# First pair of q and k through another queue and in float32, and the bias table's copies split in two, in an attention and feed-forward kernel

## The chip, the core and the metric

The kernel runs on one core of one Trainium2 chip. A core has a matrix engine (TensorE, called PE in the profile, its weight loads PEld), VectorE (DVE), ScalarE (ACT), GpSimd (POOL) and SyncE (SP), each with an instruction queue of its own, and 16 DMA engines that they share. The metric is the time of one execution on the device in microseconds (us), the lower the better. Times before and after are medians of several runs.

## The reference

Attention with a relative-position bias, over 8 batches, 8 heads, 576 positions and 64 numbers a head, and then a feed-forward stage over the 4608 tokens of 512 numbers:

```python
scores = scale * np.matmul(q, k.transpose(0, 1, 3, 2))
bias = bias_table[bucket]                    # 32 buckets x 8 heads, bucket depends on |i - j|
scores = scores + bias.transpose(2, 0, 1)[None, :, :, :]
attn = np.exp(scores - np.max(scores, axis=-1, keepdims=True))
attn = attn / (np.sum(attn, axis=-1, keepdims=True) + 1e-09)
x = np.matmul(attn, v)                       # heads side by side: 4608 x 512
h = x @ w_in                                 # 512 -> 2048
out = np.maximum(0.01 * h, h) @ w_out        # 2048 -> 512
```

All inputs and the output are float32. Beyond a distance of 127 the bucket, and so the bias, is the same for all.

## The kernel before, in words

The work is cut into 32 items, one for each batch and pair of heads (`items`, L244). The loop at L485 goes through them in order; item n's scores are made, item n-1's are multiplied with v, item n+1's q and k are turned, and pieces of the feed-forward stage (`moe`, L449) are strewn between, as soon as four pairs of a batch have given finished tokens. The order on each engine is that of the program text (`manual_schedule`, L68): an engine that waits for one instruction holds up all that stand behind it.

An item takes these steps:

- `load_qk` (L108) brings q and k of some heads by a DMA of GpSimd's queue, which casts to bfloat16 on the way, into `qn` and `kn`: 96 partitions, 6 rows of each head in a partition. `load_v` (L130) does the same for v.
- `pair_rows` (L251) sets the two heads of a pair side by side in a tile `pr`, with one VectorE copy for q and one for k (L256).
- `turned_pair` (L266) turns `pr` with six small matmuls (L272) into PSUM; `transpose_k` (L289) and `transpose_q` (L283) copy that into `kt` and `qt` (L291 on VectorE; L286 on ScalarE for the first pair), and `apart` (L276) makes a masked copy of the last 64 columns on VectorE (L278).
- `qk_mm` (L294) multiplies, `exp_band` (L315) takes the exponential on ScalarE (L319, L321, L326), and `band` (L330) multiplies the result on VectorE by a band of factors around the diagonal (L344): the bias as exp(bias - last bias), which is 1 outside of the band. For items 0 and 1 the bands come late: `bands(0)` stands at L540, near the end of the loop's second round, followed by `av(0, 0)` and `av(0, 1)`, and `bands(1)` at L550.
- `av` (L346) multiplies with v into one PSUM tile `ps_o` (one buffer), takes the reciprocal (L362) and scales (L363) on VectorE.

The factors come from the bias table. `tabT` is loaded on SyncE's queue (L170). VectorE negates its last column (`negc`, L182), ScalarE takes the exponential (`e8`, L183), and VectorE spreads the 32 values over a row `ub` of 512 places: one copy for the first 16 (L186), 15 copies for the runs of the others (L189), and one mirrored copy (L194). The row goes to DRAM as `u_row` (L200, SyncE), and from there three sorts of loads on SyncE's queue bring it back with one place's shift in each partition: `hk` for heads 0 and 1 (L202), `hk4` in two halves (L209, for the last 64 keys of every head, used by `band` with u = 5), and `hk` for heads 2 to 7 (L202).

`spin(k)` (L471) issues k matmuls on a tile of zeros, whose result is not used. The program has `spin(11)` ahead of the first pair (L479) and `spin(5)` behind its transposes (L484). ScalarE's first instructions are a table load and an exponential of one number (L85).

Of the kernel before, what the change touches and what calls it, by code (L numbers as in the profile page):

```python
# [10 lines left out]
FP32 = mybir.dt.float32  # L11
BF16 = mybir.dt.bfloat16
# [6 lines left out]
def bucket_runs(n_buckets, max_distance, seq):  # L19

    half = n_buckets // 2
    n = np.arange(seq)
    lr = np.log(np.maximum(n, 1).astype(np.float32) / half) / np.log(max_distance / half)
    large = np.minimum(half + (lr * (half - 1)).astype(np.int32), n_buckets - 1)
    bucket = np.where(n < half, n, large)
    assert (bucket[max_distance:] == n_buckets - 1).all()
    runs = []
    for d in range(max_distance):
        u = int(bucket[d])
        if runs and runs[-1][0] == u:  # L30
            runs[-1][2] = d
        else:
            runs.append([u, d, d])
    return runs
# [3 lines left out]
def kernel(  # L38
# [69 lines left out]
    def load_qk(b, h0, h1):  # L108
        i = b % NBUF
        for src, dst in ((q, qn[i]), (k, kn[i])):  # L110
            nc.gpsimd.dma_start(
                out=dst[0:RQ, h0:h1, :, :].rearrange("r h c d -> r h (c d)"),
                in_=src[b, h0:h1, :, :].rearrange("h (r c) d -> r h (c d)", c=NC),
            )
# [51 lines left out]
    for e in range(2):  # L166
        nc.vector.memset(own[e * D : (e + 1) * D, e, :], 1.0)
    tabT = per.tile([H, NB], FP32, name="tabT")
    with nc.allow_non_contiguous_dma(reason="a table of 256 numbers"):
        nc.sync.dma_start(out=tabT, in_=bias_table.rearrange("u h -> h u"))  # L170
    load_qk(0, 0, 2)
    make_identity(nc, ident)


# [8 lines left out]
    nc.scalar.activation(e8, tabT, AF.Exp, bias=negc[:, 0:1], scale=1.0)  # L183
    C0 = 2 * P - 1
    small = NB // 2
    nc.vector.tensor_copy(out=ub[:, C0 : C0 + small], in_=e8[:, 0:small])  # L186
    for u, lo, hi in bucket_runs(NB, BAND, S):
        if lo >= small:
            nc.vector.tensor_copy(  # L189
                out=ub[:, C0 + lo : C0 + hi + 1],  # L190
                in_=e8[:, u : u + 1].to_broadcast([H, hi - lo + 1]),
            )
    row = ub[:, :]
    nc.vector.tensor_copy(  # L194
        out=ub[:, C0 - BAND + 1 : C0],
        in_=bass.AP(tensor=row.tensor, offset=row.offset + C0 + BAND - 1,
                    ap=[list(row.ap[0]), [-1, BAND - 1]]),
    )
    udr = nc.dram_tensor("u_row", [H, UW], BF16, kind="Internal")
    nc.sync.dma_start(out=udr.ap(), in_=ub)  # L200
    def load_hk(h0, h1):
        nc.sync.dma_start(  # L202
            out=hk[:, h0:h1, :],
            in_=bass.AP(tensor=udr, offset=h0 * UW, ap=[[1, P], [UW, h1 - h0], [1, BW]]),
        )

    load_hk(0, 2)
    for e in range(2):
        nc.sync.dma_start(  # L209
            out=hk4[e * SL : (e + 1) * SL, :, :],  # L210
            in_=bass.AP(tensor=udr, offset=e * UW + SL + P, ap=[[1, SL], [2 * UW, n_pairs], [1, P + SL]]),
        )
    load_hk(2, H)

    def mirrored(t, lo, hi):

# [3 lines left out]
        ap[-1][0] = -1  # L220
        return bass.AP(tensor=v.tensor, offset=v.offset + hi - lo - 1, ap=ap)

    load_qk(0, 2, 4)
    load_qk(0, 4, 6)
    clear_edges(nc.vector, 1)
    load_v(0, 0, 2, True)
    load_qk(0, 6, H)
    load_v(0, 2, H, False)
# [22 lines left out]
    def pair_rows(n):  # L251

        b, p = items[n]
        t = prs[n] = pr_pool.tile([RQ, 2, NC, 2 * D], BF16, name="pr")
        for j, src in enumerate((qn, kn)):
            nc.vector.tensor_copy(out=t[:, j, :, :].rearrange("r c (e d) -> r c e d", e=2),  # L256
                                  in_=src[b % NBUF][0:RQ, 2 * p : 2 * p + 2, :, :].rearrange("r e c d -> r c e d"))

    def by_dma(n):
        return n >= 2 * n_pairs + 2  # L260
# [125 lines left out]

    def ffn_in(T):
        t0 = T * TT
        gt = gts[T] = gt_pool.tile([P, n_fc, TT], BF16, name="gt")
        for f in range(n_fc):  # L390
            pm = ps_m_pool.tile([P, TT], FP32, name="pm1", tag="m")
            for c in range(n_cc):
                nc.tensor.matmul(pm, lhsT=w_in_sb[:, c, f * P : (f + 1) * P], rhs=xT[c][:, t0 : t0 + TT],  # L393
                                 start=(c == 0), stop=(c == n_cc - 1))
            nc.scalar.activation(gt[:, f, :], pm, AF.Prelu, bias=0.0, scale=1.0, alpha=0.01)
            yield
# [79 lines left out]
        for u in range(NJ + 2):  # L476
            band(n, u)

    spin(11)  # L479

    pair_rows(0)
    transpose_k(0)
    transpose_q(0)
    spin(5)  # L484
    for n in range(N + 1):  # L485
        live = n < N
        if live:
            b, p = items[n]
            if n == 0:
                load_w_in(0)  # L490
                load_v(1, 0, H, False)
                load_w_in(1)
                load_w_out(0)
                load_w_out(1)
            elif 0 < b < B - 1:
                if p < 2:
                    load_qk(b + 1, 4 * p, 4 * p + 4)
                if p > 0:
                    load_v_part(b + 1, p - 1)
            if n + 1 < N and not by_dma(n + 1):  # L500
                pair_rows(n + 1)
            if n + AHEAD < N and by_dma(n + AHEAD):
                pair_rows(n + AHEAD)
                turn_by_dma(n + AHEAD)
            ps_a, ps_b = qk_mm(n, 0), qk_mm(n, 1)
            exp_band(n, 0, ps_a)
# [78 lines left out]
```

## Time and profile before

| what | value |
|---|---|
| runs | 391.61, 393.40, 393.59 us; median 393.4 us |
| span of the profiled execution, first to last instruction | 435.3 us |
| mean granted TensorE clock in it | 0.852 |
| PE, PEld busy | 421.2 us (97%), 199.4 us (46%) |
| DVE, ACT, POOL busy | 209.3 us (48%), 242.2 us (56%), 69.0 us (16%) |
| DMA queue q0 (GpSimd's) | 53664 packets, 18.36 MB, 40.5% of the 16 engines' span |
| DMA queue q1 (SyncE's) | 49912 packets, 21.02 MB, 26.8% |

For the profiled execution only the span is given; it stands for its own time, and it is 41.9 us above the median of the runs. The page of the profile divides the span into 40 slices and lists busy time, queues and groups of instructions. The timeline lists instructions by their start, in us from the span's start, with the time that they took; where one row stands for several instructions, xN is their number and the time is from the start of the first to the end of the last, as far as they follow each other. In brackets stands how long the engine sat idle before, and what ended that. "SPq" is SyncE's queue issuing a DMA; "KB, us" in a row on a DMA is the size at its destination and the time from the issue to the landing. The chain of waits is followed back from the last instruction to what released it.

### The profile page before, as it was taken

How to read it: one execution, taken by the hardware profiler on the slowest of the kernel's cores; microseconds unless marked ns; L12 is line 12 of the kernel's file. 1: busy time of each engine (PE TensorE's matmuls, PEld its weight loads, DVE VectorE, ACT ScalarE, POOL GpSimd, SP SyncE). 2: the span in 40 equal slices, each digit the busy share in tenths (PEclk: the TensorE clock that was granted, in tenths of full speed). 3: DMA queues.
4: the chain of work that ended last, by engine and by line, in shares of the span. 5: the costliest groups of instructions: out<-in, count | busy, mean ns of one | idle time of the engine just before them, and what ended most of it. 6: DMA issues, size and time to landing. Idle time of an engine off the chain costs nothing.

```text
span 435.3 us, 8219 instructions
## 1 busy us (share of the span) xinstructions
PE 421.2 (97%) x3384; PEld 199.4 (46%) x3384; DVE 209.3 (48%) x551; ACT 242.2 (56%) x343; POOL 69.0 (16%) x100
## 2 busy tenths in 40 slices
PE   8777999999999999999999999999999999999996
PEld 3445555444444444444444444444444454444442
DVE  6588557764556455555555455545554320000111
ACT  4776776576645666476646764676457713354000
POOL 8834230420051002400060004000000000000000
PEclk9888888888888888888888888888888888888888
DMA  8999992999289714974399349522422010000111
GB/s 107 194 196 197 206 168 42 106 131 146 64 82 172 113 27 81 185 123 44 68 152 171 44 68 98 115 37 54 60 65 17 24 43 24 26 24 0 74 48 72
DMA packets 103613, 39.89 MB, mean 92 GB/s; under 512 B 82576, under 2 KB 97944, under 8 KB 103576
## 3 DMA queue, kind: packets, MB, share of 16 engines
q0 software_dynamic: 53664, 18.36, 40.5%
q1 hardware_dynamic: 49912, 21.02, 26.8%
q8 instruction: 26, 0.43, 0.4%
q14 instruction: 11, 0.09, 0.1%
HBM read 37.68 MB, written 9.45 MB: 108 GB/s over the span
## 4 chain that ended last, share of the span: by engine, by line
PE 91%; DVE 5%; ACT 2%; issue 1%; ACTq 0%
PE ps_o L357 9%; PE ps_s L301 7%; PE ps_o L359 2%; PE ps_w L473 2%; PE ps_s L305 2%; PE ps_s L308 2%; DVE opair L363 1%; DVE at_113 L344 1%; PE pm_2157 L404 1%; PE pm_4504 L404 1%; PE pm_3930 L404 1%; PE pm_1566 L404 1%; PE pm_3339 L404 1%; PE pm_2748 L404 1%; PE pm_3191 L404 1%
## 5 line engine op out<-in xcount | busy, mean ns | idle before, releaser
L393 PEld LDWEIGHTS <-w_in_sb 128*128 128x128 bf16 x576 | 55.9, 104 | 75.6 <-issue 8.3
L404 PEld LDWEIGHTS <-gt 128*128 128x128 bf16 x576 | 54.2, 104 | 78.1 <-issue 15.0
L319 ACT ACTIVATE at_114<-ps_s 128x1024 bf16<-128x1024 f32 x64 | 62.9, 1023 | 29.4 <-PE ps_s L301 29.2
L319 ACT ACTIVATE at_113<-ps_s 128x1024 bf16<-128x1024 f32 x64 | 62.6, 1022 | 14.3 <-PE ps_s L301 14.1
L344 DVE TENSOR_TENSOR at_114<-at_114,hk 128x512 bf16<-128x512 bf16 (+1 forms) x64 | 32.2, 506 | 38.4 <-ACT at_114 L319 30.1
L344 DVE TENSOR_TENSOR at_113<-at_113,hk 128x512 bf16<-128x512 bf16 (+1 forms) x64 | 32.0, 506 | 37.9 <-ACT at_113 L319 33.7
L357 PEld LDWEIGHTS <-at_114 128*128 128x128 bf16 x640 | 29.4, 100 | 12.9 <-DVE opair L363 3.1
L357 PEld LDWEIGHTS <-at_113 128*128 128x128 bf16 x640 | 28.9, 100 | 12.6 <-DVE opair L363 3.9
L363 DVE TENSOR_TENSOR opair<-ps_o,rcp 128x320 bf16<-128x320 f32 x64 | 31.5, 491 | 2.2
L119 POOL DMA_DIRECT2D vn_107<-in_v_dram x12 | 10.7, 907 | 99.0 <-PE ps_o L359 98.9
L119 POOL DMA_DIRECT2D vn_106<-in_v_dram x12 | 10.6, 892 | 83.9 <-PE ps_o L359 79.5
L301 PE MATMUL ps_s<-qt,kt_111 64*128 64x512 bf16 x128 | 21.4, 405 | 1.0 <-ACT at_113 L321 0.4
L301 PE MATMUL ps_s<-qt,kt_110 64*128 64x512 bf16 x128 | 21.1, 403 | 0.7 <-ACT at_113 L319 0.5
L362 DVE RECIPROCAL rcp<-ps_o 128x5 f32<-128x5 f32 x64 | 12.2, 190 | 17.0 <-PE ps_o L359 17.0
L357 PE MATMUL ps_o<-vn_106,at_114 128*128 128x65 bf16 x320 | 15.7, 198 | 2.2 <-DVE opair L363 1.5
L357 PE MATMUL ps_o<-vn_106,at_113 128*128 128x65 bf16 x320 | 15.5, 198 | 2.3 <-DVE opair L363 2.1
L359 PEld LDWEIGHTS <-at_1_116 128*128 128x128 bf16 x160 | 15.9, 99 | 0.0
L359 PEld LDWEIGHTS <-at_0_115 128*128 128x128 bf16 x160 | 15.9, 99 | 0.0
L357 PE MATMUL ps_o<-vn_107,at_114 128*128 128x65 bf16 x320 | 15.2, 198 | 0.3 <-DVE opair L363 0.3
L357 PE MATMUL ps_o<-vn_107,at_113 128*128 128x65 bf16 x320 | 15.2, 198 | 0.2 <-DVE opair L363 0.2
L321 ACT ACTIVATE at_113<-ps_s 128x512 bf16<-128x512 f32 x16 | 9.5, 595 | 10.4 <-PE ps_s L305 10.4
L286 DVE COPY qt<-tu 128x576 bf16<-128x576 bf16 x22 | 14.2, 647 | 0.0
(879 smaller groups left out, 824.0 us busy)
## 6 DMA issues: line engine op xcount, KB each, us to landing
out_dram<-y SPq DMA_DIRECT2D x36, 256.0 KB, 2.2
w_in_sb<-in_moe_w_in_dram POOLq DMA_DIRECT2D x2, 1024.0 KB, 13.7
vn_107<-in_v_dram POOLq DMA_DIRECT2D x16, 128.0 KB, 5.7
w_out_sb<-in_moe_w_out_dram POOLq DMA_DIRECT2D x2, 1024.0 KB, 16.4
qn_102<-in_q_dram POOLq DMA_DIRECT2D x6, 288.0 KB, 12.5
kn_104<-in_k_dram POOLq DMA_DIRECT2D x6, 288.0 KB, 14.4
qn_103<-in_q_dram POOLq DMA_DIRECT2D x6, 288.0 KB, 7.4
kn_105<-in_k_dram POOLq DMA_DIRECT2D x6, 288.0 KB, 9.5
```

What stands on the lines that cost most here:

```text
L119: nc.gpsimd.dma_start(out=vn[i][:, c, :, 0:D], in_=v[b, :, c * P : (c + 1) * P, :].rearrange("h s d -> s h d"),)
L286: copy(out=qt[:, 0:S].rearrange("p (r c) -> p r c", c=NC), in_=turned_pair(n, 0))
L301: nc.tensor.matmul(ps[:, e, :], lhsT=kt[r, u * P : (u + 1) * P], rhs=qt[r, 0:512], start=True, stop=True)
L319: nc.scalar.activation(at[:, :, u, 0:512], ps, AF.Exp, scale=scale)
L321: nc.scalar.activation(at[:, :, :, 512:S].rearrange("p e c i -> p c e i"), ps[:, 0, :].rearrange("p (c e i) -> p c e i", e=2, i=SL), AF.Ex ...
L344: nc.vector.tensor_tensor(out=o, in0=o, in1=m, op=ALU.mult)
L357: nc.tensor.matmul(ps[:, ic, :], lhsT=at[:, o : o + P], rhs=vn[i][:, c, 2 * p + e, :], start=(c == 0), stop=False)
L359: nc.tensor.matmul(ps[:, ic, :], lhsT=at4[:, ic * P : (ic + 1) * P], rhs=v4[i][:, p, e, :], start=False, stop=True)
L362: nc.vector.reciprocal(rcp, ps[:, :, D : D + 1])
L363: nc.vector.tensor_tensor(out=opair[:, :, e * D : (e + 1) * D], in0=ps[:, :, 0:D], in1=rcp.to_broadcast([P, NJ + 1, D]), op=ALU.mult)
L393: nc.tensor.matmul(pm, lhsT=w_in_sb[:, c, f * P : (f + 1) * P], rhs=xT[c][:, t0 : t0 + TT], start=(c == 0), stop=(c == n_cc - 1))
L404: nc.tensor.matmul(pm, lhsT=gt[:, f, ts * P : (ts + 1) * P], rhs=w_out_sb[:, f, :], start=(f == 0), stop=(f == n_fc - 1))
```

## The change

- The first pair's q and k (heads 0 and 1 of batch 0) no longer pass through GpSimd's queue and `qn`, `kn`. Two DMAs on SyncE's queue bring them as float32 into a tile `qkf`, k first, which shares its buffers with the feed-forward stage's `gt`. `first_rows` takes the place of `pair_rows(0)`: VectorE sets k side by side and casts it, ScalarE does so for q.
- GpSimd's first load is now that of heads 2 and 3; all its later issues keep their order.
- The bias table's load moves from SyncE's queue to ScalarE's.
- The table's 17 copies are split. `table_first`, behind `first_rows`, makes the first one and four of the runs; `table_rest`, in the loop's first round behind `pair_rows(1)`, makes the other eleven, the mirrored copy, the store of `u_row` and the loads of `hk` and `hk4`. `clear_edges` for the second buffer (two small memsets on VectorE) moves behind it.
- `spin(11)` becomes `spin(7)`.

```diff
     tabT = per.tile([H, NB], FP32, name="tabT")
+    qkf = gt_pool.tile([P, 2, 2, NC * D], FP32, name="qkf", tag="gt")
+    for j, src in ((1, k), (0, q)):
+        nc.sync.dma_start(
+            out=qkf[0:RQ, j, :, :],
+            in_=src[0, 0:2, :, :].rearrange("h (r c) d -> r h (c d)", c=NC),
+        )
     with nc.allow_non_contiguous_dma(reason="a table of 256 numbers"):
-        nc.sync.dma_start(out=tabT, in_=bias_table.rearrange("u h -> h u"))
-    load_qk(0, 0, 2)
+        nc.scalar.dma_start(out=tabT, in_=bias_table.rearrange("u h -> h u"))
+    load_qk(0, 2, 4)
     make_identity(nc, ident)
...
-    nc.vector.tensor_copy(out=ub[:, C0 : C0 + small], in_=e8[:, 0:small])
-    for u, lo, hi in bucket_runs(NB, BAND, S):
-        if lo >= small:
+    udr = nc.dram_tensor("u_row", [H, UW], BF16, kind="Internal")
+    runs = [r for r in bucket_runs(NB, BAND, S) if r[1] >= small]
+
+    def table_runs(some):
+        for u, lo, hi in some:
             nc.vector.tensor_copy(
                 out=ub[:, C0 + lo : C0 + hi + 1],
                 in_=e8[:, u : u + 1].to_broadcast([H, hi - lo + 1]),
             )
-    row = ub[:, :]
-    nc.vector.tensor_copy(
-        out=ub[:, C0 - BAND + 1 : C0],
-        in_=bass.AP(tensor=row.tensor, offset=row.offset + C0 + BAND - 1,
-                    ap=[list(row.ap[0]), [-1, BAND - 1]]),
-    )
-    udr = nc.dram_tensor("u_row", [H, UW], BF16, kind="Internal")
-    nc.sync.dma_start(out=udr.ap(), in_=ub)
+
+    def table_first():
+        nc.vector.tensor_copy(out=ub[:, C0 : C0 + small], in_=e8[:, 0:small])
+        table_runs(runs[:4])
+
+    def table_rest():
+        table_runs(runs[4:])
+        row = ub[:, :]
+        nc.vector.tensor_copy(
+            out=ub[:, C0 - BAND + 1 : C0],
+            in_=bass.AP(tensor=row.tensor, offset=row.offset + C0 + BAND - 1,
+                        ap=[list(row.ap[0]), [-1, BAND - 1]]),
+        )
+        nc.sync.dma_start(out=udr.ap(), in_=ub)
+        load_hk(0, 2)
+        for e in range(2):
+            nc.sync.dma_start(
+                out=hk4[e * SL : (e + 1) * SL, :, :],
+                in_=bass.AP(tensor=udr, offset=e * UW + SL + P, ap=[[1, SL], [2 * UW, n_pairs], [1, P + SL]]),
+            )
+        load_hk(2, H)
...
-    load_hk(0, 2)
-    for e in range(2):
-        nc.sync.dma_start(
-            out=hk4[e * SL : (e + 1) * SL, :, :],
-            in_=bass.AP(tensor=udr, offset=e * UW + SL + P, ap=[[1, SL], [2 * UW, n_pairs], [1, P + SL]]),
-        )
-    load_hk(2, H)
...
-    load_qk(0, 2, 4)
     load_qk(0, 4, 6)
-    clear_edges(nc.vector, 1)
...
+    def first_rows():
+
+        t = prs[0] = pr_pool.tile([RQ, 2, NC, 2 * D], BF16, name="pr")
+        for j, copy in ((1, nc.vector.tensor_copy), (0, nc.scalar.copy)):
+            copy(out=t[:, j, :, :].rearrange("r c (e d) -> r c e d", e=2),
+                 in_=qkf[0:RQ, j, :, :].rearrange("r e (c d) -> r c e d", c=NC))
...
-        gt = gts[T] = gt_pool.tile([P, n_fc, TT], BF16, name="gt")
+        gt = gts[T] = gt_pool.tile([P, n_fc, TT], BF16, name="gt", tag="gt")
...
-    spin(11)
-
-    pair_rows(0)
+    spin(7)
+
+    first_rows()
+    table_first()
     transpose_k(0)
     transpose_q(0)
     spin(5)
...
                 pair_rows(n + 1)
+            if n == 0:
+                table_rest()
+                clear_edges(nc.vector, 1)
```

## The prediction

> **What bounds the kernel now.** I read the table of stages first, to see where the change can matter at all, then the chain of waits for the first 43 us, then the timeline of the first 24 us with the queues' issues and landings. The change touches nothing behind the first two items, so I need to know whether a shift there reaches the end.
>
> ```profile
> span 435.3 us, 8219 instructions
> ```
>
> ```profile
> 30.00:40.00 10.00, 7.70 (x142) 5.30 (x141) 8.62 (x26) 9.15 (x11) 4.54 (x6) 0.85 1.71 183
> ...
> 100.00:200.00 100.00, 100.00 (x829) 47.12 (x827) 54.41 (x139) 62.55 (x90) 14.90 (x20) 0.85 0.82 107
> ```
>
> The columns are the stretch, its length, busy us of PE, PEld, DVE, ACT and POOL, the granted clock, DMA. From 100 us on PE is never idle, and nothing in that stage is changed. Between 30 and 40 us DVE and ACT are the busy ones, and PE waits. So the kernel is a start-up of some 43 us, in which the engines wait for each other, and a long stage bound by PE. A start-up that is shorter by x ends the kernel earlier by x, since the long stage takes what it takes. The chain confirms it (start, us, what):
>
> ```profile
> 1.24 4.87 PE ps_w L473 x11
> ...
> 8.39 1.95 ACT at_113 L319 x2
> ...
> 42.51 0.38 DVE xT_97 L382
> 42.93 0.38 PE pm_780 L393
> ```
>
> It runs through the eleven spins, the first exponentials and on to the first feed-forward matmul at 42.93 without a gap. The span is 41.9 us above the median of 393.4: at the granted clock of 0.85, the 388 us from 42.93 to the end hold about 58 us that a full clock would not need, so I take the timed runs to be granted more. The start-up hardly depends on that: it is ACT, DVE and DMA time. I therefore work with differences in the profiled start-up, and add them to 393.4.
>
> **When the first pair is ready.** These rows of the timeline and of the landings carry it:
>
> ```profile
> 0.75 1.28 ACT L85 ACT_TABLE_LOAD   x1 [0.75 <-PEq L569]
> 0.76 0.39 SPq L170 DMA_DIRECT2D tabT<-in_bias_table_dram  x1
> ...
> 1.31 0.76 POOL L111 DMA_DIRECT2D qn_102<-in_q_dram  x1 [0.85 <-POOLq L569]
> 2.06 0.66 POOL L111 DMA_DIRECT2D kn_104<-in_k_dram  x1
> ...
> 3.32 0.08 DVE L182 TENSOR_SCALAR negc<-tabT 8x1 f32<-8x1 f32 x1
> 3.45 0.32 ACT L183 ACTIVATE e_136<-tabT,negc 8x32 bf16<-8x32 f32 x1 [1.20 <-DVE negc L182]
> 3.80 0.17 DVE L186 COPY ub<-e_136 8x16 bf16<-8x16 bf16 x1 [0.40 <-ACT e_136 L183]
> 3.88 1.28 DVE L189 COPY ub<-e_136 8x3 bf16<-8x3 bf16 x15
> 5.20 0.19 DVE L194 COPY ub<-ub 8x127 bf16<-8x127 bf16 x1
> 5.46 0.28 DVE L256 COPY pr<-qn_102 96x768 bf16<-96x768 bf16 x1
> 5.67 0.33 DVE L256 COPY pr<-kn_104 96x768 bf16<-96x768 bf16 x1
> 6.06 0.70 PE L272 MATMUL ps_t<-ident,pr 96*128 96x96 bf16 x12
> 6.60 1.41 PE L473 MATMUL ps_w<-junk 128*128 128x512 bf16 x5
> 6.80 0.64 ACT L286 COPY qt<-ps_t 128x576 bf16<-128x576 bf16 x1 [3.03 <-PE ps_t L272]
> 7.88 0.49 DVE L256 COPY pr<-kn_104 96x768 bf16<-96x768 bf16 x1
> 7.95 0.64 PE L301 MATMUL ps_s<-qt,kt_110 64*128 64x512 bf16 x4
> ```
>
> ```profile
> kn_104<-in_k_dram POOLq DMA_DIRECT2D x1, 144.0 KB, 3.3
> hk<-u_row SPq DMA_DIRECT2D x1, 192.0 KB, 4.6
> hk_101<-u_row SPq DMA_DIRECT2D x1, 96.0 KB, 6.0
> hk<-u_row SPq DMA_DIRECT2D x1, 576.0 KB, 7.8
> ```
>
> Three things end together at the first transposes (6.06): k lands at 2.06 + 3.3 = 5.36; DVE finishes the table's copies at 5.39 and sets the pair side by side until 6.00; the eleven spins end near 6.1. To gain anything all three must go, and the change takes all three. (The two short memsets that it also moves cost less than 0.2 us and go with the copies.)
>
> *Loads.* k is issued at 0.76 in place of `tabT`, and q behind it at about 1.2 (0.4 us of issue, as the `tabT` row has). No row shows a float32 load of 288 KB by SP. From below, `tabT` (1 KB) landed in at most 3.32 - 0.76 = 2.56; from above, the 192 KB of `hk` took 4.6 among other traffic. I take 3.3, the row of the same tensors, which read the same 288 KB: k lands at 4.1, q at 4.5 (3.8 to 5.8).
>
> *The table ahead of them.* `negc` on DVE and `e8` on ACT stand ahead of the two side-by-side copies, so those wait for `tabT`, now issued by ACT. Two bounds: if ACT's queue issues while the table load still runs, `tabT` lands at about 0.75 + 2.56 = 3.3; if it waits until the load and the one-number exponential are done (2.2), at 4.8. One row speaks for the first:
>
> ```profile
> L286 ACTq EVENT_SEMAPHORE  x2: 17/17/17, 14.1 to 31.4; - x2
> ...
> 13.50 1.94 ACT L319 ACTIVATE at_114<-ps_s 128x1024 bf16<-128x1024 f32 x2
> ```
>
> At 14.1 ACT's queue took a semaphore, for a copy still to come, while the engine was busy with exponentials. I take 3.5, a little late for the two large loads that share the DMA engines. `e8` is then done at 3.95, before q has landed, and the wait costs nothing.
>
> *Side by side.* The bf16 copy of k's shape took 0.33 on DVE (5.67); with twice the bytes to read I take 0.65 (from 0.33 to the 1.0 to which a 576-element copy out of PSUM, at 0.75, would scale). k is ready at 4.75 and not the last. q on ACT: 0.64 for 576 elements in the 6.80 row, so 0.85 for 768 (0.64 to 0.97, half of the two 1024-element exponentials in the chain's row at 8.39): ready at 4.5 + 0.85 = **5.35**, between 3.8 + 0.64 = 4.45 and 5.8 + 0.97 = 6.8.
>
> *From there to the first scores.* Before, q's six transposes began at about 6.33 (half of the twelve behind 6.06), and the scores at 7.95: 1.62 for transposes, copy, mask and spins. `table_first`'s five short copies (0.17 + 4 x 0.085 = 0.5) run on DVE while PE turns k and ACT copies q, and end at 5.25; their cover is that DVE's next work is k's copy at 5.3. If PE is still at its slow rate during the transposes, as the spins' 4.87 / 11 = 0.44 each was against 1.41 / 5 = 0.28 later, add 0.25. So scores at 5.35 + 0.05 + 1.62 + 0.25 = 7.3 in place of 7.95: **0.65 gained**, between 1.8 gained (4.45) and 0.55 lost (6.8).
>
> **Whether the gain lasts: the bias rows.** The table's rest now runs behind `pair_rows(1)`, and all that SP did with the row comes later:
>
> ```profile
> 5.41 0.28 SPq L200 DMA_DIRECT2D u_row<-ub  x1
> 8.40 0.41 SPq L202 DMA_DIRECT2D hk<-u_row  x1
> 8.86 1.33 SPq L209 DMA_DIRECT2D hk_101<-u_row  x2
> 10.23 0.61 SPq L202 DMA_DIRECT2D hk<-u_row  x1
> ```
>
> ```profile
> 11.17 0.76 DVE L291 COPY kt_111<-ps_t 128x576 bf16<-128x576 bf16 x1 [1.15 <-PE ps_t L272]
> ...
> 15.74 0.81 POOL L111 DMA_DIRECT2D qn_103<-in_q_dram  x1
> 16.00 0.23 DVE L278 TENSOR_TENSOR qt<-qt,own 128x128 bf16<-128x128 bf16 x1 [3.08 <-ACT qt L286]
> ...
> 17.22 1.76 DVE L344 TENSOR_TENSOR at_113<-at_113,hk 128x512 bf16<-128x512 bf16 x4
> 18.89 0.25 DVE L344 TENSOR_TENSOR at_0_115<-at_0_115,hk_101 128x192 bf16<-128x192 bf16 x1
> ...
> 23.05 1.75 DVE L344 TENSOR_TENSOR at_114<-at_114,hk 128x512 bf16<-128x512 bf16 x4
> ```
>
> Before, `pair_rows(1)` ended at 8.37, which is 0.42 behind the first scores; after, at 7.7. Eleven copies of 1.28 / 15 = 0.085 and the mirrored one (0.19) are 1.15: `u_row` is issued at 8.85, **3.45 later** than at 5.41. (The 1.15 itself lies on DVE in a time in which it waited: it idled 1.15 us ahead of 11.17 and 3.1 us ahead of 16.0.) With the same distances behind it:
>
> - `hk` of heads 0, 1 landed at 8.40 + 4.6 = 13.0, now 16.45. Wanted by the bands of item 0 at 17.22, now 16.55: just in time.
> - the second half of `hk4` was issued at about 9.5 and landed at 15.5, now 18.95. Wanted at 18.89, now 18.25: **0.7 late**.
> - `hk` of heads 2 to 7 landed at 18.0, now 21.5. Wanted at 23.05: in time.
>
> The wait for `hk4` is a new one, on DVE. Behind it stand the reciprocal and scaling of item 0, and for these waits PE, which has one PSUM tile for `ps_o`. So the gain of 0.65 is given back, and 18.95 for 18.89 is a loss of about 0.1. The sum: -0.65 + 0.7, rounded up to **+0.1**: 393.5. GpSimd's later loads all move forward by the two issues taken away (0.76 + 0.66 = 1.4); none of them is in the chain, so that gains nothing, but it changes what the rows' loads collide with. The float32 tile writes 2 x 144 KB more, at a time when the DMA engines have only that and the next pair in hand.
>
> **The rivals.**
>
> 1. *The rows come in time and the gain stays.* For it: `hk4`'s 96 KB took 6.0 us while `hk`'s 192 KB, begun first, took 4.6, so most of that was collision. At 4.6 it lands at 12.95 + 4.6 = 17.55, before 18.25. Then -0.65: 392.75, and 391.6 with the early end of q's bounds. Against it: GpSimd's loads are as many in that stretch as before.
> 2. *The rows come much later.* This is the side on which the change is slower, by one mechanism: SP's four DMAs behind `u_row` run 3.45 later, into GpSimd's 576 KB loads of the next batch, begun at 15.74 before and 1.4 earlier now. It decides as soon as `hk4` takes over 6 us; at 7.8, as the large `hk` took, it lands at 20.75, 1.85 after 18.89: 395.3. Against it: SP's packets get a share beside GpSimd's however many of those wait.
> 3. *PE stays at its slow rate.* Seven spins last 7 x 0.44 = 3.1 us and end at 4.3, and PE then idles until k is ready at 4.75; before, 4.9 us without a gap stood ahead of the fast rate. If it comes only after the second spins, those take 5 x 0.44 = 2.2 from 5.9, the scores begin at 8.1 and take 0.2 more: the first exponential at 8.75 for 8.39, +0.35; with the next seven spins slow too, up to +1.6. Time: 394.1 (393.75 to 395.0). The Trainium skill, "TensorE: Matmul & The Clock Gate", Part 1: The HAM clock gate, says that the full clock is given after a busy window of about 3.4 us, and that the windows run free of the kernel's start. The trace of before agrees (4.9 us of spins before the fast rate); by the rule seven spins cannot fill a window alone, which speaks for this rival. That the transposes follow within half a microsecond speaks against it.
> 4. *The first inputs come late.* `tabT` at 4.8: `e8` at 5.3, q ready at 6.15, scores at 7.85, `u_row` 4.0 later, `hk4` at 19.5: +0.6, 394.0. With q landing at 5.8 instead: scores at 8.5, `hk4` at 20.15, +1.25, 394.65. In either case the change does not do what it says.
>
> **How the numbers follow.** Chances: forecast 0.40, rival 1 0.27, rival 2 0.13, rival 3 0.10, rival 4 0.10. The three runs before lie 2.0 us apart, so each case spreads by about one. Half a per cent, about what a measurement of this kernel can tell from no change, is 2.0 us: below 391.4 or above 395.4. Below lie a good third of rival 1 (0.11) and 0.06 of the rest: 0.17. Above lie half of rival 2 (0.07) and 0.10 of the forecast, rivals 3 and 4: 0.17. The rest, 0.66, is no change. The range goes from the early end of rival 1, 391.5, to rival 2's price, 395.3.
>
> **What would show it.** First scores (L301) at 7.3 and not 7.95; `negc` at about 3.5 (at 4.8 rival 4); spins at 0.44 and 0.28 as before, the second five shorter than 1.5 us (2.2: rival 3); the `u_row` issue at 8.85; and DVE idle ahead of the band with `hk4`, released by that DMA, at about 18.95 (no such wait: rival 1; past 20: rival 2). The prediction is wrong as a whole if the feed-forward's first matmul moves by another amount than the first scores and the bands do, or if the stage behind it changes its length.

## The result and the profile after

| | before | changed |
|---|---|---|
| runs | 18 | 18 |
| median | 393.75 us | 396.22 us |
| lowest to highest | 391.61 to 397.91 | 393.12 to 399.94 |
| ratio of the two | | 1.0057, 95% interval 1.0033 to 1.0082 |

The changed kernel is slower by 0.57%, some 2.2 us. The forecast was 393.5 with a range to 395.3.

The profile of before on which the prediction rests was taken at a granted clock of 0.85 throughout. The profile of the changed kernel has 0.987, as most timed runs of both kernels do. To compare like with like I took one more profile of before (0.986), and set the changed kernel against that one below. One run of before (970.5 us) and one of the kernel kept warm below (486.6 us, at a clock of 0.754 throughout) lie far off all the others, and no comparison rests on them.

First the start of the changed kernel, from its timeline:

```profile
0.92 0.57 ACTq L176 DMA_DIRECT2D tabT<-in_bias_table_dram  x1
1.21 0.43 SPq L171 DMA_DIRECT2D qkf<-in_q_dram  x1
...
1.23 3.17 PE L492 MATMUL ps_w<-junk 128*128 128x512 bf16 x7 [1.23 <-DVE junk L162]
...
4.83 0.14 DVE L188 TENSOR_SCALAR negc<-tabT 8x1 f32<-8x1 f32 x1 [1.44 <-DMA tabT<-in_bias_table_dram]
4.90 0.75 DVE L275 CAST pr<-qkf 96x768 bf16<-96x768 f32 x1
...
5.83 0.83 ACT L275 CAST pr<-qkf 96x768 bf16<-96x768 f32 x1 [0.50 <-DMA qkf<-in_q_dram]
...
6.98 1.25 PE L492 MATMUL ps_w<-junk 128*128 128x512 bf16 x5
...
8.16 0.60 PE L320 MATMUL ps_s<-qt,kt 64*128 64x512 bf16 x4
```

ScalarE's queue issues the table's load at 0.92, while the table load of the engine itself runs until 2.03: the queue does run ahead, as forecast. Yet the 1 KB lands only at 4.83, 3.9 us later (at most 2.6 before). It now has two loads of 288 KB beside it and another queue; no run separates the two. q lands at 5.83, 4.6 us after its issue. The first scores stand at 8.16, where before had 7.95 (7.93 in its profile at 0.986). So the start gains nothing.

Then the bias rows, with VectorE's bands of item 1 and the last load of `hk`:

```profile
10.31 0.34 SPq L214 DMA_DIRECT2D u_row<-ub  x1
...
14.21 0.82 POOL L111 DMA_DIRECT2D qn<-in_q_dram  x1
14.89 0.60 SPq L224 DMA_DIRECT2D hk<-u_row  x1
...
15.01 0.78 POOL L111 DMA_DIRECT2D kn<-in_k_dram  x1
...
26.15 1.93 DVE L363 TENSOR_TENSOR at<-at,hk 128x512 bf16<-128x512 bf16 x5 [2.77 <-DMA hk<-u_row]
```

The landings of those loads (KB at the destination, us from issue to landing):

```profile
hk<-u_row SPq DMA_DIRECT2D x1, 576.0 KB, 11.2
hk<-u_row SPq DMA_DIRECT2D x1, 192.0 KB, 3.3
hk<-u_row SPq DMA_DIRECT2D x2, 96.0 KB, 3.8
```

Here is the loss of this execution. The last load is issued between GpSimd's two 576 KB loads of the next batch and takes 11.2 us, where it took 7.8 before. It lands at 26.1, and VectorE has sat idle for 2.77 us. The chain of waits of the changed kernel runs through the table's eleven late copies, the store of the row and this load:

```profile
8.82 1.25 DVE ub L197 x11
10.31 2.73 DMA u_row<-ub
...
14.89 11.23 DMA hk<-u_row
26.15 0.90 DVE at L363 x2
```

`hk` of heads 0 and 1 and `hk4` land in 3.3 and 3.8 us, earlier than forecast, and nobody waits for them. PE idles along with VectorE. In the stage from 20 to 30 us (columns as in the prediction) the changed kernel has

```profile
20.00:30.00 10.00, 5.77 (x69) 3.45 (x69) 5.32 (x16) 2.61 (x4) 2.07 (x4) 0.60 1.19 221
```

and the new profile of before has

```profile
20.00:30.00 10.00, 8.77 (x105) 6.31 (x106) 6.44 (x20) 4.47 (x5) 4.98 (x7) 0.51 1.25 205
```

ACT's 2.61 busy us against 4.47 are the work that is late. The eighth column is news, too: in both kernels TensorE's granted clock is near 0.5 in this stage. The profile at 0.85 could not show that. More on it below.

The prediction asked whether the first feed-forward matmul moves as the bands do. In the two profiles at 0.986 and 0.987 the bands of item 1 start at 23.69 and 26.15 (2.5 later), the first matmul with the weights at 43.2 and 45.3 (2.1 later), and the spans are 393.2 and 394.3. Of the 2.1 us the two spans show 1.1, and the medians, with 2.5, all. From the first such matmul to the end it takes 350.0 and 349.0 us, and 349.0 to 350.7 in thirteen of the sixteen profiles at the usual clock, whatever the start-up was: what comes later in the start-up ends later by as much, to within that scatter. In the other three it takes 352.5 to 353.5, for a wait near 90 us that is shown below, with the held loads and eleven spins.

### The profile page after: what moved, and what is told of

It is laid out like the page before. It is cut to its first block, busy times and chain, and to the rows that moved or that the text cites. A ratio compares the mean times of both kernels' runs of the same rounds, so it can differ in the third digit from the quotient of the medians.

```text
span 394.3 us, 8214 instructions
## 1 busy us (share of the span) xinstructions
PE 375.1 (95%) x3380; PEld 188.0 (48%) x3380; DVE 209.0 (53%) x550; ACT 243.0 (62%) x344; POOL 67.4 (17%) x98
## 3 DMA queue, kind: packets, MB, share of 16 engines
HBM read 37.68 MB, written 9.45 MB: 120 GB/s over the span
## 4 chain that ended last, share of the span: by engine, by line
PE 83%; DVE 7%; DMA 6%; ACT 2%; issue 1%; SPq 1%; ACTq 0%
PE pm L412 32%; PE pm L423 30%; PE ps_o L376 9%; PE ps_s L320 7%; DMA hk<-u_row 3%; PE ps_o L378 2%; DVE at L363 2%; DMA xT<-opair 1%; PE ps_s L324 1%; PE ps_s L327 1%; DMA qkf<-in_q_dram 1%; DVE opair L382 1%; ACT at L338 1%; DVE kt L310 1%; DVE pr L268 1%
## 5 line engine op out<-in xcount | busy, mean ns | idle before, releaser
L338 ACT ACTIVATE at<-ps_s 128x1024 bf16<-128x1024 f32 x128 | 125.4, 1023 | 35.6 <-PE ps_s L320 35.6
L423 PE MATMUL pm<-w_out_sb,gt 128*128 128x512 bf16 x576 | 139.9, 380 | 0.0
L412 PE MATMUL pm<-xT,w_in_sb 128*128 128x512 bf16 x576 | 138.6, 379 | 0.8 <-DVE xT L401 0.6
L414 ACT ACTIVATE gt<-pm 128x512 bf16<-128x512 f32 x144 | 86.1, 598 | 66.0 <-PE pm L412 62.6
L363 DVE TENSOR_TENSOR at<-at,hk 128x768 bf16<-128x768 bf16 (+3 forms) x160 | 71.7, 456 | 90.9 <-ACT at L338 49.2
L423 PEld LDWEIGHTS <-gt 128*128 128x128 bf16 x576 | 50.5, 98 | 65.8 <-issue 13.8
L376 PEld LDWEIGHTS <-at 128*128 128x128 bf16 x1280 | 55.6, 99 | 25.4 <-DVE opair L382 7.2
L376 PE MATMUL ps_o<-vn,at 128*128 128x65 bf16 x1280 | 59.3, 195 | 7.5 <-DVE opair L382 4.3
L428 DVE COPY y<-pm 128x512 f32<-128x512 f32 x36 | 24.7, 687 | 67.6 <-PE pm L423 67.5
L378 PE MATMUL ps_o<-v,at 128*128 128x65 bf16 x320 | 52.3, 195 | 0.0
L320 PE MATMUL ps_s<-qt,kt 64*128 64x512 bf16 x256 | 40.8, 389 | 2.0 <-ACT at L338 0.7
L378 PEld LDWEIGHTS <-at 128*128 128x128 bf16 x320 | 31.5, 98 | 0.0
L340 ACT ACTIVATE at<-ps_s 128x512 bf16<-128x512 f32 x32 | 19.1, 595 | 10.3 <-PE ps_s L324 10.2
L381 DVE RECIPROCAL rcp<-ps_o 128x5 f32<-128x5 f32 x64 | 12.2, 191 | 11.2 <-PE ps_o L378 11.1
L305 DVE COPY qt<-tu 128x576 bf16<-128x576 bf16 x22 | 14.2, 645 | 0.0
## 6 DMA issues: line engine op xcount, KB each, us to landing
qn<-in_q_dram POOLq DMA_DIRECT2D x12, 288.0 KB, 10.1
w_in_sb<-in_moe_w_in_dram POOLq DMA_DIRECT2D x2, 1024.0 KB, 15.4
hk<-u_row SPq DMA_DIRECT2D x1, 576.0 KB, 11.2
```

The lines of the kernel that those rows point to most:

```text
L320: nc.tensor.matmul(ps[:, e, :], lhsT=kt[r, u * P : (u + 1) * P], rhs=qt[r, 0:512], start=True, stop=True)
L338: nc.scalar.activation(at[:, :, u, 0:512], ps, AF.Exp, scale=scale)
L363: nc.vector.tensor_tensor(out=o, in0=o, in1=m, op=ALU.mult)
L376: nc.tensor.matmul(ps[:, ic, :], lhsT=at[:, o : o + P], rhs=vn[i][:, c, 2 * p + e, :], start=(c == 0), stop=False)
L378: nc.tensor.matmul(ps[:, ic, :], lhsT=at4[:, ic * P : (ic + 1) * P], rhs=v4[i][:, p, e, :], start=False, stop=True)
L423: nc.tensor.matmul(pm, lhsT=gt[:, f, ts * P : (ts + 1) * P], rhs=w_out_sb[:, f, :], start=(f == 0), stop=(f == n_fc - 1))
```

## The experiments

Each ratio is to the kernel before, in runs on the same chip, with its 95% interval.

**Before once more, for a profile at the usual clock.** No edit.

> The kernel before, unchanged, for a profile at the clock that most timed runs have (the profile at hand has 0.85 throughout). Theory: first scores at 7.9, the bands of item 1 at 23.0 to 23.7 with no wait on hk, the first matmul of the feed-forward at 43 to 44.5; a clock of 0.98 to 1.0. Rival (the start-up before depends on the clock, too): the first feed-forward matmul at 45 or later, so that little of the 3.8 us by which the changed kernel's is later comes of the change.

One run: 395.0 us. First scores at 7.93, and no wait on `hk`:

```profile
23.69 1.92 DVE L344 TENSOR_TENSOR at<-at,hk 128x512 bf16<-128x512 bf16 x5
```

The first feed-forward matmul comes at 43.2. The rival fell.

**The whole table early, the rest of the change as it is.**

```diff
     first_rows()
     table_first()
+    table_rest()
+    clear_edges(nc.vector, 1)
     transpose_k(0)
...
-            if n == 0:
-                table_rest()
-                clear_edges(nc.vector, 1)
```

> The changed kernel, with the rest of the table's copies, the store of the row and its loads put back ahead of the first pair's transposes; the float32 loads, the table's load on ScalarE's queue and the seven spins stay. Theory (the loss is the late load of hk for heads 2 to 7): first scores at 9.0 to 9.3 (1.2 later than 8.16, since kt's copy now stands behind the copies), the row's store issued at 7.3 to 7.6 in place of 10.31, the last hk load landed by 22 in place of 26.1, no wait of DVE on hk ahead of the bands of item 1 or one under 1 us; time 394.3 to 395.0, faster than the changed kernel and up to 0.3% slower than before. Rival A (the loss is the start: inputs that land late, the seven spins): the start is the worst of all here, so 397 or more, slower than the changed kernel. Rival B (the loss is a slow TensorE clock after the shorter spins): as the changed kernel, 396.

395.13 us, just above what was expected, ratio 1.0025 (0.9996 to 1.0054). The row is stored at 6.38, the last `hk` load issued at 11.61 and landed at 20.2, and there is no wait. Although the first scores are late (9.45, with the first exponential at 10.1), the loss is no larger than that of the whole change; by the medians it is about half of it. That speaks for the late load as one part and leaves another part in the start.

**The split of the table alone.** The edit is the change's `table_first` and `table_rest` in the kernel before, with `table_first()` ahead of `pair_rows(0)`.

> The kernel before, with one part alone: the table's copies split, the first five ahead of the first pair, the rest with the row's store and loads behind the second pair's side-by-side copies. GpSimd loads the first pair, SyncE the table, eleven spins. Theory: first scores at 7.9 as before; the row's store at 9.5, the last hk load issued at 14 and landed at 22.5 to 25; DVE waits 0 to 2 us on it ahead of the bands of item 1 (wanted at 23.05); time 394.0 to 396.0, that is 0.1 to 0.6% slower than before. Rival A (the start is the loss): no wait that counts, 393.2 to 394.0, the same as before. Rival B (spins): 393.7 as before, since the eleven spins stand.

395.99 us, ratio 1.0036 (1.0009 to 1.0062): slower by itself. Only the place of the wait differs from what I expected. With the first pair ready a little earlier (first scores at 7.49), VectorE waits for the rows already at the bands of item 0, once for `hk` of heads 0 and 1 and once for `hk4`:

```profile
17.52 1.76 DVE L351 TENSOR_TENSOR at<-at,hk 128x512 bf16<-128x512 bf16 x4 [0.86 <-DMA hk<-u_row]
20.38 0.26 DVE L351 TENSOR_TENSOR at<-at,hk 128x192 bf16<-128x192 bf16 x1 [1.09 <-DMA hk<-u_row]
```

This is the wait for `hk4` that the prediction forecast for the changed kernel, here at 20.38.

**GpSimd's later loads held until the last row has landed.**

```diff
-    load_qk(1, 0, H)
+    hold = per.tile([P, 1], BF16, name="hold")
...
-            if n == 0:
-                load_w_in(0)
...
             if n == 0:
                 table_rest()
                 clear_edges(nc.vector, 1)
+                nc.gpsimd.tensor_copy(out=hold, in_=hk[:, H - 1, 0:1])
+                load_qk(1, 0, H)
+                load_w_in(0)
+                load_v(1, 0, H, False)
...
```

> The changed kernel, with GpSimd's loads of the next batch and of the weights held until the last hk load has landed, by a copy of one column of hk on GpSimd ahead of them. Theory (the last hk load takes 11.2 us because it collides with the next batch's 576 KB loads): issued at 14.9 as before, it lands at 19 to 21, DVE does not wait on it ahead of the bands of item 1, and these start at 23.1 to 23.4 in place of 26.15; the later weights may take part of that back; time 393.5 to 395.5. Rival (the load is slow by itself, whatever GpSimd loads): it lands at 25 or later still, and the time is 396 or more.

The load's part came out as the theory said:

```profile
hk<-u_row SPq DMA_DIRECT2D x1, 576.0 KB, 5.5
hk<-u_row SPq DMA_DIRECT2D x1, 192.0 KB, 4.6
hk<-u_row SPq DMA_DIRECT2D x2, 96.0 KB, 4.9
```

Issued at 13.85, the last load lands at 19.4, and there is no wait. With the loads held and an issue as late as in the changed kernel, at 15.0 and 15.1 in two runs further below, it took 4.7 and 5.5. So 11.2 us were a collision with GpSimd's loads. The time was a miss: 396.38 us, ratio 1.0052 (1.0027 to 1.0077). The bands of item 1 start at 25.03 and not at 23.4, with no wait ahead of them. The timeline shows why, in the spins and the first scores:

```profile
6.99 1.46 PE L492 MATMUL ps_w<-junk 128*128 128x512 bf16 x5
8.38 1.04 PE L320 MATMUL ps_s<-qt,kt 64*128 64x512 bf16 x4
...
9.81 1.48 PE L492 MATMUL ps_w<-junk 128*128 128x512 bf16 x3
```

Three spins take 1.48 where the changed kernel's profile has 0.81. The stages of the profile with the loads held show TensorE back at half its clock there (the eighth column):

```profile
8.00:11.00 3.00, 3.00 (x15) 0.89 (x13) 2.77 (x19) 1.94 (x2) 2.96 (x4) 0.50 1.50 148
```

**The last load cut in two, heads 2 and 3 first.**

```diff
         load_hk(0, 2)
+        load_hk(2, 4)
...
-        load_hk(2, H)
+        load_hk(4, H)
```

> The changed kernel, with the load of hk for heads 2 to 7 cut in two: heads 2 and 3 as the second load, ahead of both of hk4, and heads 4 to 7 last. Theory: heads 2 and 3 land by 18, hk4 by 19.5, so that the bands of items 0 and 1 wait at most 0.5 us, and the bands of item 1 start at 23.1 to 23.6 in place of 26.15; heads 4 to 7 land at 24 to 26, wanted by the bands of item 2 at 25.6; time 393.8 to 395.0, 0.3 to 0.6% faster than the changed kernel. Rival A (the start is the loss): 396, as the changed kernel. Rival B (TensorE's slow clock from 22 to 32 us comes of the seven spins and not of the wait): the slow clock stays and the time is 395 to 396.

399.81 us, ratio 1.014 (1.0093 to 1.0188): the worst of all, though its profile, of a run of 394.4, has no wait. Its six timed runs are 394.4, 396.9, 399.1, 400.6, 401.4 and 401.4. Two more profiles followed:

> The kernel with the load of hk for heads 2 to 7 cut in two once more, for a second profile: its timed runs went from 394.4, the profiled one, to 401.4. Theory (late loads of rows, by amounts that vary): in a run of 397 or more the profile shows a wait of DVE on hk of heads 4 to 7 of 2 us or more ahead of the bands of item 2 (at 26.6 in the first profile). Rival (the clock alone): no such wait, and two windows more at half the clock.

394.2 us, again no wait.

> The kernel with the hk load cut in two, a third profile, since both so far are of runs at 394 while four timed runs took 399 to 401. Theory: in a run of 397 or more a wait on hk or hk4 of 2 us or more. Rival (the clock alone): no such wait.

403.8 us, and this time:

```profile
25.24 0.26 DVE L364 TENSOR_TENSOR at<-at,hk 128x192 bf16<-128x192 bf16 x1 [4.12 <-DMA hk<-u_row]
```

with the landings

```profile
hk<-u_row SPq DMA_DIRECT2D x2, 192.0 KB, 4.7
hk<-u_row SPq DMA_DIRECT2D x1, 384.0 KB, 12.9
hk<-u_row SPq DMA_DIRECT2D x2, 96.0 KB, 9.1
```

Now `hk4`, pushed back by one load, falls into the collision: 9.1 us, where it took 5.3 and 4.8 in the two good runs, and a wait of 4.1 us. The row had been stored at 10.92 here and at 9.88 and 9.73 in those. One microsecond decides whether a load of SyncE's goes ahead of GpSimd's burst at 14.1 or into it. The wait is not the whole difference: the first feed-forward matmul comes at 49.5 (43.2 and 42.7 in the good runs), and behind it this run takes another 3 us more (352.5 for 349.4 and 349.7).

**Eleven spins in the changed kernel.**

```diff
-    spin(7)
+    spin(11)
```

> The changed kernel with eleven spins again in place of seven; all else stays. In the runs so far TensorE's slow first rate ended at 4.5 to 4.9 us in two of the kernels with seven spins and at 9.1 and 9.9 in two others, whose first scores came 0.7 to 1.1 us later. Theory (seven spins are too few for a window that runs free, on top of the late load of hk): the slow rate ends between 4.0 and 7.5, the first scores stand at 8.0 to 8.4 whatever the window, the wait on hk ahead of the bands of item 1 stays at 2 to 3 us; time 395.2 to 396.0, that is 0.2 to 0.8 us under the changed kernel. Rival (the spins do not matter): 396.2 as the changed kernel.

396.67 us, ratio 1.0043 (1.0016 to 1.0069). The run does not settle the spins' part: the expected gain over the changed kernel is smaller than the interval. Its runs fall into two groups, 393.8 to 394.6 (4 runs) and 395.9 to 398.5 (8). The profile, of the first group, has the row stored at 9.77, the last load issued at 13.93 and landed at 22.2, and no wait. A second profile:

> The changed kernel with eleven spins once more: its timed runs fall into 393.8 to 394.6 and 395.9 to 398.5, and the profiled one, 394.6, had no wait on hk. Theory: in a run of 396 or more DVE waits on hk, by 1.5 us or more; in one under 395 it does not. Rival (the clock): no wait in either, and more windows at half the clock in the slower one.

394.0 us, row stored at 9.70, last load landed at 21.1, no wait. The wait of 2 to 3 us that I expected is in neither profile. That both runs without a wait are fast fits the theory, but no profile falls into the slower group, so whether its runs have the wait is not shown.

**The changed kernel once more.**

> The changed kernel once more, for a second profile. Theory (the last hk load lands late by an amount that varies with the traffic of the moment): issued at 14 to 15, it lands between 21 and 27; if past 23.4, DVE waits on it ahead of the bands of item 1 and the first feed-forward matmul comes at 44.5 or later, if not, at 43 to 44. Rival (the loss lies elsewhere): the first feed-forward matmul stands at 45 whether DVE waits there or not.

397.9 us. The last load, issued at 15.48, takes 11.2 us again:

```profile
26.73 1.94 DVE L363 TENSOR_TENSOR at<-at,hk 128x512 bf16<-128x512 bf16 x5 [1.87 <-DMA hk<-u_row]
```

First scores at 9.51 this time (8.16 in the first profile), first feed-forward matmul at 46.25. The spins differ, too: the second five take 2.33 us here and 1.25 in the first profile.

**Seven spins in the kernel before.**

```diff
-    spin(11)
+    spin(7)
```

> The kernel before with seven spins in place of eleven, and nothing else. Theory: the first transposes still begin at 6.0 (k lands at 5.4), but in most executions the slow rate lasts until 8 to 10 us, so that the first exponentials come 0 to 1.3 us later; time 394.2 to 395.0, 0.1 to 0.3% over before. Rival (the spins do not matter): 393.9 as before.

395.92 us, ratio 1.0035 (1.0013 to 1.0057). Seven spins alone cost more than I gave them. The timeline of PE:

```profile
1.23 3.17 PE L473 MATMUL ps_w<-junk 128*128 128x512 bf16 x7 [1.23 <-DVE junk L162]
6.04 1.14 PE L272 MATMUL ps_t<-ident,pr 96*128 96x96 bf16 x12 [1.65 <-DVE pr L256]
6.98 2.33 PE L473 MATMUL ps_w<-junk 128*128 128x512 bf16 x5
9.25 1.02 PE L301 MATMUL ps_s<-qt,kt 64*128 64x512 bf16 x4
```

PE idles 1.65 us ahead of the transposes. They take 1.14 (0.88 in the profile of before at 0.986), the second five spins 2.33 (1.24), and the first scores come at 9.25 (7.93).

**The loads alone: the change with table and spins as before.** The edit is that of the whole table early, and `spin(11)`.

> The changed kernel with the whole table ahead of the first pair's transposes and eleven spins: of the change there stay the float32 loads by SyncE, the side-by-side copies out of them, and the table's load on ScalarE's queue. Theory (late hk load and too few spins are the loss; the loads bring nothing): q lands at 5.8 as in the changed kernel, first scores at 8.2 to 8.9, no wait on hk, time 393.9 to 394.8, 0 to 0.2% over before and under the changed kernel by 1.5 or more. Rival (the loads themselves cost): 395.5 or more.

393.92 us, ratio 0.9999 (0.9969 to 1.0029). The float32 loads, the copies out of them and ScalarE's load of the table cost nothing and bring nothing that this interval shows. First scores at 8.45.

**The held loads and eleven spins.** Two edits from above together.

> The changed kernel with GpSimd's later loads held until the last hk load has landed, and eleven spins; nothing against the slow clock of 20 to 32 us. Theory (the late hk load and the seven spins are the change's own two costs; that slow clock is one that before has as well): first scores at 8.1 to 8.5, no wait on hk, time as before within 0.15%, 393.6 to 394.6, and 0.4 to 0.6% under the changed kernel. Rival (the three unused matmuls made up for a cost of the change in the run that had all three): 395.2 or more.

394.58 us, ratio 1.0007 (0.9982 to 1.0032): back at before. The last load takes 4.7 us, and the bands of item 1 start without a wait:

```profile
23.18 1.92 DVE L363 TENSOR_TENSOR at<-at,hk 128x512 bf16<-128x512 bf16 x5
```

With the loads of rows out of the collision and the spins back, nothing of the loss is left that can be measured. The profile is of the slowest of the twelve runs, 397.8 us, and yet its first feed-forward matmul comes at 42.5. What made this run slow lies behind that, where PE waits for a DMA of SyncE's queue that transposes:

```profile
91.05 0.58 PE L412 MATMUL pm<-xT,w_in_sb 128*128 128x512 bf16 x1 [3.11 <-DMA xT<-opair]
```

The granted clock falls to half for 3.4 us at the same time. Of the sixteen profiles at the usual clock the three with the longest stage behind the start-up (352.5 to 353.5) are the three in which this wait takes 2.1 to 3.1 us and the clock falls; in the other thirteen it takes 0.2 to 1.8 us and the clock stays up. So a single run that is 3 us slow need not have a late `hk`.

**The kernel before kept warm.** Not a part of the change, but a test of the slow clock at 20 to 32 us.

```diff
             bands(0)
             av(0, 0)
+            keep(3)
             av(0, 1)
+            keep(3)
...
+    def keep(k):
+        t = ps_m_pool.tile([P, 512], FP32, name="ps_k", tag="m")
+        for _ in range(k):
+            nc.tensor.matmul(t, lhsT=junk[:, 0:P], rhs=junk, start=True, stop=True)
```

> The kernel before with three more unused matmuls behind each of the two v products of item 0 (L541, L542), where PE waits 0.8 us for VectorE's scaling. The timed runs of before have a mean granted clock from 0.983 to 1.000, and the times at 1.000 are 392.5 to 393.4. Theory (a slow TensorE clock between 20 and 32 us, given when PE idles there, costs 0.6 us for each window of 3.4): the clock is 0.995 or more in most runs, time 392.7 to 393.5, 0.1 to 0.3% under before. Rival (the clock is not decided there): 393.9 or more, by up to 0.5 us of added matmuls.

393.1 us, ratio 0.9979 (0.9964 to 0.9994): faster than before, with six matmuls more. In eleven of its twelve runs the mean granted clock is 0.997 or more. Its only profile is of the twelfth, at 0.754, and shows nothing of this stage at the usual clock. Of 98 timed runs of before beside the experiments, 14 have 0.9975 or more and a median of 392.8, and 43 have at most 0.9885 and a median of 395.0. In the changed kernel 11 of 18 lie in the lower group, with a median of 396.4, and none in the upper.

**All three undone in the changed kernel.** Held loads, eleven spins and `keep`.

> The changed kernel with three things taken out of the way: GpSimd's later loads held until the last hk load has landed, eleven spins, and three unused matmuls behind each v product of item 0 against the slow clock. Theory (these three are the whole loss): first scores at 8.1 to 8.4, no wait on hk, the clock 0.995 or more, time 392.9 to 394.0, that is 0.6 to 0.8% under the changed kernel. Rival (something else of the change costs): 395 or more.

393.59 us, ratio 0.9987 (0.9955 to 1.0019). In its profile the clock stays up:

```profile
20.00:30.00 10.00, 7.89 (x118) 4.62 (x118) 7.90 (x23) 5.56 (x7) 7.72 (x10) 1.00 0.93 138
```

**A version meant to beat both.** The kernel kept warm, with k alone as float32 by SyncE behind the table's load, cast by ScalarE; q by GpSimd; the table whole and early; ten spins.

```diff
-    load_qk(0, 0, 2)
+    kf = gt_pool.tile([P, 2, NC * D], FP32, name="kf", tag="gt")
+    nc.sync.dma_start(out=kf[0:RQ, :, :], in_=k[0, 0:2, :, :].rearrange("h (r c) d -> r h (c d)", c=NC))
+    nc.gpsimd.dma_start(
+        out=qn[0][0:RQ, 0:2, :, :].rearrange("r h c d -> r h (c d)"),
+        in_=q[0, 0:2, :, :].rearrange("h (r c) d -> r h (c d)", c=NC),
+    )
...
-    spin(11)
+    spin(10)
```

> The kernel before kept warm (three unused matmuls behind each v product of item 0), with k alone of the first pair as float32 by SyncE behind the table's load, cast by ScalarE; q by GpSimd, the table whole and early, ten spins. Theory (two large loads at once land late, one does not; the row's loads stay early): k lands at 4.3 to 4.8, the first scores at 7.3 to 7.6 in place of 7.9 to 8.2, no wait on hk, the clock 0.997 or more; time 392.4 to 393.0, 0.3 to 0.5% under before. Rival (the start-up is set behind the first scores): 393.1, as the kernel kept warm alone.

393.12 us, ratio 0.9964 (0.9935 to 0.9994). It beats both kernels, but it cannot be told from the kernel kept warm alone, and its first scores stand at 7.95. k is set side by side at 5.3, no later than expected, and then the transposes and spins still run at the slow rate (1.17 and 1.57 us).

## Why the prediction was wrong, point by point

- *A shift of the start-up ends the kernel by as much.* Right, within the scatter of the long stage (349.0 to 350.7): 2.5 at the bands, 2.1 at the feed-forward, 2.5 in the medians. Two readings were off without effect on the sum: from 42.93 to the end of that profile are 392.4 us, not 388, and the first matmul with the weights stands at 41.53; the one at 42.93 is a later one.
- *ScalarE's queue issues while the engine loads its table.* Right (0.92). *`tabT` lands at 3.5:* wrong, 4.83. I had given the two large loads 0.2 us of effect; it came 1.3 later than that. For q it lay under q's landing. k, landed at 3.9, had to wait for it on VectorE until 4.90.
- *k lands at 4.1, q at 4.5:* k 0.75 + 3.1 = 3.9, right; q 5.8, the upper bound. I took the time of one load for the second of two that share the engines with each other and with GpSimd's next. *Side-by-side copies of 0.65 and 0.85:* 0.75 and 0.83. *0.65 gained at the first scores:* 0.21 lost. The loads alone (ratio 0.9999) confirm, to within 0.3%, that the gain is absent and that nothing else hides in them.
- *`u_row` 3.45 later, at 8.85:* 10.31 (9.4 to 10.9 in the other kernels with the split). The second pair is side by side 1.1 later than forecast, at 8.82, and the copies behind it take 1.49 in place of 1.15. The first scores alone do not set the store: one of the profiles with eleven spins also has them at 8.16, and stores the row at 9.70. The first row here is of the changed kernel, the second of that one:

```profile
8.74 1.32 DVE L197 COPY ub<-e 8x4 bf16<-8x4 bf16 x11
8.58 0.88 DVE L197 COPY ub<-e 8x4 bf16<-8x4 bf16 x11
```

The same copies took 1.32 us in both profiles of the changed kernel and in both with held loads and eleven spins, and 0.88 to 1.12 in the others with the split. Why is not shown.
- ***`hk` of heads 2 to 7 lands at 21.5, in time.* This is the step that failed.** I shifted its 7.8 us unchanged into a time with other traffic. It landed at 26.1 in the first profile, 4.6 later than forecast: 1.2 by the later issue (14.89 for 13.68) and 3.4 by the longer time. It took 11.2, in both profiles of the changed kernel, and 4.7 to 5.5 with GpSimd held. The 1.55 us that the load had to spare became a wait of 2.8 and 1.9 us. Rival 2 named this very collision, with GpSimd's 576 KB loads, but put it at `hk4`, which is issued 0.6 us before it and got through in 3.8. The argument against that rival, that SyncE's packets get a share beside GpSimd's however many wait, did not keep the larger load from losing about 6 us. And the sign for rival 1, no wait for `hk4`, came true in a kernel that was slower. *`hk4` 0.7 late:* wrong for the changed kernel, though seen with the split alone and, by 4.1 us, with the load in two.
- *Seven spins (rival 3, chance 0.10, +0.35 to +1.6).* The price was fair: alone they cost 0.35% (0.13 to 0.57), about 1.4 us. The chance was too low. Among eight profiles with seven spins the first exponential came at 8.6 once, at 9.0 to 9.3 twice, and at 9.7 to 10.2 five times; among ten with eleven or ten, never past 8.9, whichever way the first pair was loaded. My argument against it, that the transposes follow within half a microsecond, was worth little: k was set side by side 0.9 later than forecast, and PE idles 1.3 us. In the traces the full clock is first granted at 3.9 to 4.9 us in three of the eight, behind 3.4 us in which PE was busy for 77 to 93%, and in two of these three it falls back to half for 3.4 us, at 7.3 and 7.9; in the other five it comes at 9.1 to 12.0. With ten or eleven spins the clock goes up at 4.0 to 7.3 and stays up until 20 us. The rule of the Trainium skill ("TensorE: Matmul & The Clock Gate", Part 1: The HAM clock gate) is a busy window of about 3.4 us, in windows that run free of the kernel's start. These runs agree with the length and with an end of the slow rate that wanders between runs of one kernel; the windows ahead of the full clock were not always filled.
- *The range, to 395.3.* I had weighed rivals 2, 3 and 4 as alternatives. They are not: the inputs came late in both profiles of the changed kernel, the last load collided in both, and in the second the spins were slow as well (first exponential at 10.15, against 8.59 in the first). A sum of two of the priced cases, 1.85 and 0.35, would have given 395.7, still half a microsecond short of the median.

On the kernel before, each of the two parts costs by itself (split alone 1.0036, seven spins alone 1.0035). In the changed kernel they do not add up that way. The ratios to before:

| changed kernel, with | seven spins | eleven spins |
|---|---|---|
| GpSimd's loads as they are | 1.0057 (1.0033 to 1.0082) | 1.0043 (1.0016 to 1.0069) |
| those loads held | 1.0052 (1.0027 to 1.0077) | 1.0007 (0.9982 to 1.0032) |
| the whole table early | 1.0025 (0.9996 to 1.0054) | 0.9999 (0.9969 to 1.0029) |

With the loads held or the spins back, but not both, no gain clears the noise; with both the time is that of before. So the two together are shown to be the loss; how it is split between them is not. In single profiles the wait goes with the store of the row: stored by 9.9 there was no wait in four profiles of the split with float32 loads, stored at 10.3 to 10.9 there was one in three, as long as GpSimd was not held. What part of the runs of the changed kernel has the wait stays open; both profiles have it.

## What to carry to other kernels

A DMA's time from issue to landing belongs to the traffic of its moment: when a load is moved, look at what the other queues issue around the new place, and price it from the slowest row there rather than shifting the old time. A load that sits well ahead of another queue's burst is worth keeping there: with the table early and eleven spins the time was that of before. And rivals that can happen in one run are not alternatives: a range that treats them so is too narrow. What they cost together has to be measured; here removing one of two costs gave nothing that could be told from noise, and removing both gave all.

## What the runs showed of the hardware that was not expected

- Moved by a microsecond, the same load of 576 KB took 7.3 to 8.3 us (issued at 13.8 to 13.9, just ahead of GpSimd's loads at 14.2 and 14.3), 11.2 (issued at 14.9 and 15.5, 0.7 and 0.9 us after the first of them) and 4.7 to 5.5 (those loads held). Being ahead is no promise, though: with the split alone it was issued at 13.7, GpSimd's loads at 15.4, and it took 10.9.
- A 1 KB load took 3.9 us on ScalarE's queue with two loads of 288 KB beside it, against at most 2.6 on SyncE's without them; which of the two did it is not separated.
- TensorE's clock falls to half in thirteen of the sixteen profiles at the usual clock, at 20 to 26 us, where PE waits on VectorE ahead of the feed-forward stage, and for 3.4 us or a multiple of it (6.8 and 10.2 in most). In the 3.4 us before it falls PE is busy for 48 to 61%, and no gap is longer than 1.0 us. Runs with some 10 us at half the clock, an estimate from the mean clocks above, take some 2 us more (medians 395.0 and 392.8). Six unused matmuls in PE's idle gaps keep it up.
- Far behind the start-up, at 89 to 97 us, PE waits for a transposing DMA. In three profiles of sixteen that wait took 2.1 to 3.1 us (0.2 to 1.8 in the others), the clock fell to half for 3.4 us at its end, and the rest of the kernel took some 3 us longer.
